# A new table of order, engine and PSUM bank for 2,542 operations of a four-layer attention kernel

## The chip, the cores and the metric

The kernel runs on one core of a Trainium2 chip. The metric is the device time of one execution in microseconds (us). The names of the engines are those of the profile: PE (TensorE matmuls), PEld (TensorE weight loads), DVE (VectorE), ACT (ScalarE), POOL (GpSimd) and SP (SyncE, which here only issues DMAs).

## The reference

Four layers run one after the other on x of 2048 tokens by 512 features. Each adds its result to x. Layers 1 and 3 are linear attention (A), layers 2 and 4 are causal attention in a window of 256 tokens (B), each with 32 heads of 16 features.

```python
def _A_ref(x, wqkv, wo):
    q, k, v = ...                      # x @ wqkv, split in 32 heads of 16
    phi = lambda t: jnp.where(t > 0, t + 1, jnp.exp(t)) + 1e-6
    pq, pk = phi(q), phi(k)
    kv = jnp.einsum("bhsd,bhse->bhde", pk, v)
    z = jnp.einsum("bhsd->bhd", pk)
    num = jnp.einsum("bhqd,bhde->bhqe", pq, kv)
    den = jnp.einsum("bhqd,bhd->bhq", pq, z)[..., None] + 1e-6
    o = num / den
    return ... o ... @ wo

def _B_ref(x, wqkv, wo):
    scores = jnp.einsum("bhqd,bhkd->bhqk", q, k) * (Dh ** -0.5)
    mask = (idx[:, None] - idx[None, :] >= 0) & (idx[:, None] - idx[None, :] < 256)
    p = _softmax(jnp.where(mask, scores, -1e9), axis=-1)
    o = jnp.einsum("bhqk,bhkd->bhqd", p, v)
    return ... o ... @ wo

x = x + _A_ref(_layernorm(x), A_wqkv, A_wo)
x = x + _B_ref(_layernorm(x), B_wqkv, B_wo)
x = x + _A_ref(_layernorm(x), A_wqkv, A_wo)
x = x + _B_ref(_layernorm(x), B_wqkv, B_wo)
```

## The kernel before

The 2048 tokens are 16 tiles of 128. x stays in SBUF (`xres`). A class `Plan` first writes down a graph of 2,542 operations. Each has a name, the engines that may run it, a function that emits its instructions, and what it reads and writes. One operation is a handful of instructions. The names that matter here:

- `x0` ... `x12`, `wAk`, `wAq`, `wAv`, `wAo`, `wBn`, `wBv`, `wBo` are the loads of x (by first tile) and of the weights, all issued by SP in `setup`. In the load list, the eighth and later ones wait for the load four places earlier in that list.
- `stats`, `aggr`, `eps`, `pow`, `xn` are the layer norm of a tile (DVE, and POOL for `pow`; `eps` on either). `T` brings the normalised tile into transposed form, by PE for a few tiles and by a DMA transposition on SP for the rest.
- `k`, `q`, `v` are the projections of an A layer, two operations a tile each; `E` (an exponential on ACT), `E1` and `phi` (DVE) follow on `k` and `q`. `g`, `gv`, `z`, `kv`, `kvm`, `M` form the state of an A layer; `den`, `rec`, `recb`, `spread`, `pqd` divide; `aout` and `res` close it.
- `bq`, `bk`, `bv` are the projections of a B layer. Their evacuations `bqe`, `bke`, `bve` may run on ACT or DVE. `kd` and `vd` are DMAs on SP that rearrange keys and values.
- `s` is a group of score matmuls into four PSUM banks, `ex` one of the two exponentials on ACT that read a pair of these banks, `mk` and `mf` the causal masks (DVE; `mf` on DVE or POOL), `pv` the product with the values, `rcp` and `div` the division, `oT` the transposition of the output, `bout` and `res` the end of the layer. There are 156 groups `s` and 312 `ex`.
- `outp` and `out` are the stores of the result, `outp` by POOL or SP.
- `fill` are ten dummy matmuls, `c..`, `zero`, `wp` are constants, clears and weight copies.

When the instructions are emitted, nothing is planned any more: `place` unpacks `TABLE`, a compressed string, and takes from it three things: one order of all operations, the engine of each operation that has a choice, and a PSUM bank for each of the 1,007 PSUM tiles. Each engine runs its operations in the order of the table, and waits with semaphores for what is not yet done. The core of it:

```python
order = [ops[raw[2 * k] + 256 * raw[2 * k + 1]] for k in range(n)]
...
    o.eng = ("PE", "ACT", "DVE", "POOL", "SP")[raw[2 * n + o.i]]
...
    x.banks = [raw[3 * n + k]]
```

An operation that opens a PSUM tile also waits for all users of the tile that held that bank before. SP executes its queue in order, so a DMA whose data isn't ready holds back the ones behind it. The DMAs that it has issued land later by themselves.

The score groups are emitted by `b_scores` (L638) and `b_far` (L677, L680). An `ex` (L648, L690) reads two banks with one instruction, through a view that steps from the first bank of the pair to the second. In the table before, the second bank of a pair is always the one after the first.

Of the kernel before, what the change touches and what calls it, by code (L numbers as in the profile page):

```python
# [11 lines left out]
P = 128  # L12
D = 512
DH = 16
S = 2048
T = 16
# [202 lines left out]
def bass_view(x, free):  # L219

    return bass.AP(x.tensor, x.offset, [x.ap[0]] + free)


class Plan:
# [398 lines left out]
    def b_scores(self, j, b, fs, key):  # L623

        K = self
# [4 lines left out]
        last = (q + ns - 1) // P  # L630
        span = lambda two, free: bass_view(K.PS[:, two[0].banks[0], :], free([512 * (two[1].banks[0] - two[0].banks[0]), 2]))

        def put(e):
            m = None
            for i, f in enumerate(fs):
                for gq in range(4):
                    rows = slice(32 * gq, 32 * gq + 32)
                    m = e.matmul(K.ps(ps[gq])[:, ns * i:ns * i + ns], K.kB[rows, j % 4, 2 * f + b, :, :], K.XQ[rows, f, q:q + ns], start=True, stop=True, tile_position=(32 * gq, 0))  # L638
            return m
# [5 lines left out]
        for h in range(2):  # L645
            def ex(e, h=h):
                i = span(ps[2 * h:2 * h + 2], lambda x: [[ns, n], x, [1, ns]])
                return e.activation(out(h, ns).rearrange("p (f g) c -> p f g c", f=n), i, ACT.Exp, bias=0.0, scale=0.25)  # L648

            self.on("ACT", "ex", ex, key + 0.01 * h, act(2 * ns * n), wr=[("P", sl, f, b, h) for f in fs], rd=[("P", sl, f) for f in fs], ps=[ps[2 * h], ps[2 * h + 1]])  # L650
# [9 lines left out]
    def b_far(self, j, key):  # L660
# [3 lines left out]
        ps = [Tile(1, "S") for _ in range(4)]  # L664
        span = lambda two, free: bass_view(K.PS[:, two[0].banks[0], :], free([512 * (two[1].banks[0] - two[0].banks[0]), 2]))

        def put(e):
            m = None
            for f in range(4):
                for b in range(2):  # L670
                    q = P * j + 64 * b
                    c = 128 * f + 64 * b
                    for gq in range(4):
                        rows = slice(32 * gq, 32 * gq + 32)
                        x = K.XQ[rows, f, q + 256:q + 320]
                        if not merged:
                            m = e.matmul(K.ps(ps[gq])[:, c:c + 64], K.kB[rows, j % 4, 2 * f + b, :, :], x, start=True, stop=True, tile_position=(32 * gq, 0))  # L677
                            continue
                        for half in range(2):
                            m = e.matmul(K.ps(ps[gq])[64 * half:64 * half + 64, c:c + 64], K.kB[rows, j % 4, 2 * f + b, 32 * half:32 * half + 32, :],  # L680
# [5 lines left out]
        for h in range(2):  # L686
            def ex(e, h=h):
                i = span(ps[2 * h:2 * h + 2], lambda x: [[128, 4], x, [64, 2], [1, 64]])
# [171 lines left out]
    r"c-qZa1K1|VvaT*P*0yciwr$(CZQHhO+qTW@CcDXcb7%hV<eVfoo0F4!@AKUGhSk+o?^{*fGyMUCh3765goc+c9E6835CI|rLPAiG2oggihztY|-3#}`C",  # L860
    r"4r=n43a|>hzijl3kWoa6p#`avO+fK1uY;ujD@Ez2SkS$&>LDpE9e8oAQe1v8a6_D$N)JZ7i0tjaUd=@c<fq38+hjCLu%LreIXx=gZ!`=YC|392gRX3jE",
    r"8s-6Ba;xXbbJY!USjp?I9C9aCKn-420Zp80tY9=m1@zK6Hc3&>dnyIY<i)AUHIJK`<CP!bC^_O<)o%ghj9zmcUi$1Y4j7Y=t3k1dhTn*aop79W;b4Py#",
    r"x`WOxo!U?>cOGEf$#LQi-BFJUPxgXItmuE7^L4%guZOoQoA9lpZPumWzvN{Fjw!EBfV!=XHU2d|(4Y=<4N6L!H|m;p0kHSC5}a023~lW+<^DHU4HgD@(",
    r"-N}%?_Ew~MLpedY&Gw>S1syz@+B~;(TS-1;7z#BLZ;Z=H72~d$@RTG*)26YbZ!F?D3BViO&1yK*+Eo4-gR3epF{Rlrn1Qk(5QUz5ZRaj+KSyU3G)k84K",
    r"s>rH{DypKWf=~#mKvb1fy@O;bxpFGH8VzHhw#urqsbVU-%Aty@5~`$%rgEyvkW!^kxl}1tTIE({RaI3@l~Gkx0jQ($KwhY;>Zt~*vZ}6XsFtdgYOQLjT",
    r"B^QU18ZR&6ow*D6xyhUs;z3I8mo4yiE6K!tBTN6HB&9rde{Ip-~#M}{cr#}sDm(CjZq=s5j=*uYM!bFW7Rk{QjJm<VVxSU)~iEM5+<mLYQDMzlhgur85",
    r"XJ|s-xPVp1@O>tlq;1n4)H=nQE3=q&BL>YKfYvrm5+wlez+%)Mm9`9aRU^QuPcvt1fDeI;OU$t?Hm!sk*9<uu9c})vBB7u0FvswOj?m;J8A~R=3n~6#|",
    r"2);OdSl1t-)=bxQS6Au$wQRoB#QbzN;!C9ouZhSMs9I;;+<N9wUEh1*p~6-t%H&=>}HsGaJGx~ZaL42+4-)C<*9mBF&OOYK(A)jf4zmBTZtmkNt})LB&",
    r";o~m=|fm)+3sEg{nTB~AX0!)Mn@uez{XYirAq-tU<ysK`gI2aG(Vr@K&=WrCB#|wB7M`IEkgYj{nN`|RaYV}UNS0B_H^-;Z5KdPTpQcR8^AsnVr;V}Y^",
    r"#c?<uBVt;W0uy5etcaDcGVWE8FeRo_bulug!i*RN>){oZ2`{S&I1w9Q6|9Q&F*9bt)OZPF;bp9Y)$o&QhAnV5&cV6Z96zf`_(gqHKP$jS*ch{7Hq4GW@",  # L870
    r"Gf4#?^Hv)hxf4wHpN#;AtK>xH5q?UQ*bJ_!mHQ@b7E_}hS#y2`d;-`jOA5Zte`5YN-7Q3z+9LXJ7X8@iVH9uw#0>)8@pk5%z$|?FXlr*jZrZ_7QjUq4H",
    r"u(9i%YNv&PRvKuqRH#7-}h|$CxUX>V*YyIZnqJ7+b|rE3go*!mYRsx8n|6iG5UGRUOyhIxLL+)Bx2RS7U!w1jEr<T#rSu7>1_^R2(BxB#KP)@EJbG7kC",
    r"4A;x62cd+-N*gEz4<RiU?d3m@SVe29;+5B9~ExEG^PRLY~OQa_AFc~yTLfcaE@)ebx0U7CdhaS%Sm0_q;M$4)pHhv1JGpAt|)x=#buAoU%-#u?NRXJR#",
    r"~PBo||?Zf@}3OC?Jyn_dDCVj%sIEyyn_qYXXQ40EkUvW0gp`Q^bB`HEmMX4zX#iH1hjN;Hx9ENGAHXX#Il$?g+2poy&XfAEW=oEuuQhjPb4=@8A!ozq3",
    r"(^5{#MYpjbJ)lhVkXlkkBFas9s1+rmN0gqJgftz+%(Rl)QXLwsT2mWpPl@RmKBgzMidIuQ>Oeo?dwhrSs4mr`yp)gf(+4a-9jOU5rB2kD3X-9&)Sa5qa",
    r"Xf(^@g#Pm=G2eYQGc38mK+76`LuxI(kVQR184&Ur$RK4TF`nbOkHRb^`IgYf{Icx8bpI>Ej^_nw3&v|7Ro|dX)6_{5>%2F(jr<+*=PxEqwTbmcF;1~NF",
    r"gZ{4N)W1P?eoRQy3~mKhPT*uHMoxwTpIB4%$PBI58*Tq@0Y`P-!YdWhpF`qsCO8l5+~~NiV4vrQ~NcjC#{|G@M4zNE$_r=oRgw*R-Gd&~y5p4$~2OL8I",
    r"v?9is#EiN4Sp9z$bkFYTnYypEgmJNiuTX&il}7Tl5#Q7S%8<LLyQq!08n0r&M@8mH(qt>?^~g@2-~oSJ{6kJO4=a~md3!)aNVIRuB~P@IF?a!wA-nhz3",
    r"kE<QtN=^UM>c07S5QXUS&VR;fwrYV$;^Ko7d$KkmM=jIEvfs1i|UQX$`D6gOl{3HLw@3=h|;6i+nE>UsL#+RuqZ{$rJfy;4cF3%OXAQ$G%+?Ts>f9}9t",
    r"xg!tcPW+xfa7C`fmH7%);eI@T2lF5v!iF7ZXUh>e5@+OK9GRnVRlZ8s=sNY_o*b2X@fIG*qj)Ms<7w1~qw{E<PJ4MD-=O^*gM0HwF2SF;6lda?e3Pnib",  # L880
    r"*{lRxg_u4ojjC>@h%R|lejcb=2~2v4{>*%!ee+Uf9B!5mACN--p;q^HXY_V+>MX$F+Ra{`3u+Mqdbj|b1aU{cPI`|=aYPnm0aK%tR*hbWRzK4hU0ld-~",
    r"gZJQ+$SvSUJtt`37I);1WXWa{~@34f!UY<=cFV@9<qd$WB5_SZT!fcs7TTIoz1%@;v^^;pIL@lwk5RXOrwQmO&!Od|to{c^v1EP_l@da8n-7&G-R7<VX",
    r"CNpKxS}BCVvgw2`B7iKEIfxy*YwJ}2Ob99?$vaY@LFc>*utrTj!#u5b*ACXwW+h=h|ka*gB4Q+~$FcsZ}&n37+f^9z0^&!wPT<=7HW;!6TaD7oZ?6p%!",
    r"cSdvI?$tx!$kDQcKa!$@mEGaBSWF@cS3sOifN^vPFB_*F+lFL#-DoST5A*=bNd?%HpvUHVV(q6hqDXAh=rJLlGYEoU=Nm5BB9i)czmX6X%l1p2uK(FMr",
    r"RHXirLQ+a9NiBV(uk@4er4n_Q9x^}%${_iH-*6g9D{r}{%$51lOXkS}dCA}LD}K%2b7?6ngJp=6k(x47W=Sn6FGFRRq?7bATjoePSt`q9xtx|Wa#m_f9",
    r"a$)grLNSI`qDt&$$R-A86>l;kd?AZ7ReGBE+b^5jFQo^R@TW6vR<;t8`&UN<f^QejFMHZiPCFiqr8<dGFCpyCut~+q_K>X@zO*#$#vN*TjYk^lv{FJ>g",
    r"xu2t8DXLX{5Ky4%sQqrG?y)rqWFA$^_XZtfz_SA7#4yB)eszOp-lvNHWP}nIU^+pG=W^GFA4=0ck1s<*+=EgYr<0$Rl|y_4H@?B3boU$)~gETsptbqx0",
    r"$l`ezBQL+Bhjx6Y|S7u4BwcCEG1g>*yRNEg<fbr)Sk57kyX-B>r#O?5L}R7cdqbXOflht-jEbKOF>)ZO$PJy#FcA$2R=PPf+`bVnUZch{|TC*4Mm(9?B",
    r"j9a;C#J#{bLTesDH^hg~{kJ91v3>`(!)1&nmT};o^vvhIYSC7>Lba*{bm(b(%AU#A6)=_mo-Csx0CG~h+T9?uj^h8}oZ_-<ISv_B0(O30m9mXus3-wmL",
    r"O@}qx^(1{w&(@3db-h@JGdJ{2eM>LV`}AZzMNiX3Oi@$J?AHhM4!ujS)wlId9p0?d>-8NSO&2#MOmrPXf2U*W*E*JdrDN+jI<Agjmg;3XqS>wY>VtZ@j",  # L890
    r";G`6je4qns-Njd=DFUWBbzAZrCy;|>OJ~<{YL+wALxgAmA<P#>d*R-KCBbyg!+j7q!a0qrj&W1SL=KFkiM_K=(r}Hd8>ca$Mp#v-yGGa^%;FqpVB|+$2",
    r"zJxs}t*UI-2>a-|2EXx+!fw==VCQPNI|P<hr~j<4rs!g-)pxnHVOC(dL+5qZ6B$rm9J5l9_5ImN~C~*2&EUeNls{pwXl=)lCL-NgHEL8B^9c6U?MHnM?",
    r"|k(xfuwOnH;hj5Xs-LQ~5mFi-S&)5r8R{Y)Lx-wZGVO?Fe;1UH#YYLnLFFgZ;wGsvVdgG~jK#nd(RO;%IUR5C+MJrlx&G@(p0)7<1X*-ReOz~nVGO)6c",
    r"*q}KV2GA&Fi)6z6D4NZDoQCHR(bX7gn3^Qr;Yg0*oZ>s2wdbnw9nwU)b2Q$KqG--8aolZA3Tg+Co&9pY#O&k;3j53qVQ8UHlHwDaOQ_!?Ag-l^H)l4(T",
    r"Obv6~yfK~4bTiL%F+0poQ`yWnNo-fs&5SV%%r3Lr>@jamQv0KsVP=_Rw!P_KCYnWNrdeo`+m7ZZv)H^d?@cFj%A7IPbazu-pEhkx9Xs08we{=-v)s%!b",
    r"IlyH!mKo_%mLHRoHZ$IeS6RxGKbAxv(Kco=gc*8-YhZ8%u=)8tTv&|8nf1{GpTG3)6?`a*Ud@Oz}C<=%uRE_T=JH8XvuysC(JE#(OfoH%x&}0tT&&`W&",
    r"PQFF{$lUbH`|V-#jp1%@K3gG_=+>vW@LM^UzD}Bjao^o5lvWkIfSk&PK3LO;(%DX1C#OTAR+Mw;}8^6Us)kA??owY$UtEY&4rpbQ{CQw4H2Z+u6plZEZ",
    r"Un+IF#Ft=KS@Z3f%kX0(}X6Wi2AvAJv>+srn%(QFIb()Kp3Y;OD9<hA*1ew*1wwXtm+8`s9O#cXl=!n`!!nG&|9uBGeh0(Od>YU}7}wxBI!YwM+UnVoL",
    r"C+8H*B&1rMk<@Sv2X3yGlwy^DPi`toXmYr?m+XVKNNob4Mezw0IU`yIkw!E!i=h)IVkzHk1+cLJYtzs+MO16g`XxG?5wyLdWhuib^f^B0j+FtgOoonaW",
    r"`L?I+ZTs30cChVZJJ`$Cy0vz_9ckCuQP#O3Hkb?U7TAThwcTd7+eP-Sy=TkW9X5~KU^m*1_P)*Qs@obigv;kbx=^mB-DDrxC$^RyZO7QncDK#%3b@Dii",  # L900
    r"rr#w*qgSXE9A=Bv38tYVsF`%cB>t4huNq0ncZWb+ZFZ)`__hbyX+nN#$L78>|uM|zOXy(Ui;F9ar^CJd&Iu7-`Vf&YkSllu*d8J`_M*p2kjwy-2P}|x!",
# [169 lines left out]
```

## Time and profile before

| what | value |
| --- | --- |
| time, median of 3 runs | 410.4 us (410.2 to 413.33) |
| span of the profiled execution | 408.2 us, 18,082 instructions, granted clock 1.000 |
| what the lowest run has beyond this span | 410.2 - 408.2 = 2.0 us |
| PE, PEld, DVE, ACT, POOL busy | 396.0, 263.4, 347.9, 344.4, 113.8 us |
| first and last `ex` of layer 2 | 62.7 to 224.4 us |
| first and last `ex` of layer 4 | 257.6 to 400.7 us |
| DMA | 37.88 MB, mean 93 GB/s |

The time of a run is a little longer than the span, which goes from the first to the last instruction of the profiled execution. Layer 1 lies ahead of the first `ex`, layer 3 mostly between 213 and 258 us, where few exponentials of scores run. A busy PE is not a PE at its peak, since matmuls are pipelined and their ends are modelled.

### The profile page before, as it was taken

The numbers are of one execution on the slowest core, as the hardware profiler recorded it, in microseconds if no ns is written. First come the engines' busy times: TensorE is split into PE (matmuls) and PEld (weight loads), VectorE is DVE, ScalarE is ACT, GpSimd is POOL, SyncE is SP. The second block draws the span as 40 slices with busy tenths as digits, with TensorE's granted clock in tenths as the row PEclk, the third lists the DMA queues.
The fourth block names the chain that finished last, engine by engine and source line by source line (L and its number), as shares of the span: only waits on it lengthen the run. The fifth ranks groups of instructions, "written<-read, shape, count | busy, mean of one in ns | idle before, by whom it ended". The sixth has DMA issues, their size and how long they took to land.

```text
span 408.2 us, 18082 instructions
## 1 busy us (share of the span) xinstructions
PE 396.0 (97%) x7997; PEld 263.4 (65%) x7997; DVE 347.9 (85%) x808; ACT 344.4 (84%) x443; POOL 113.8 (28%) x194
## 2 busy tenths in 40 slices
PE   8999999999999999999999999999999999999996
PEld 3654676666575566666666777676757766576664
DVE  5998799999998999888977789988898778876685
ACT  3655579999999999999998355999998999999992
POOL 3553632112253343330503202122123201302212
PEclk9999999999999999999999999999999999999999
DMA  8754014923242934344231100364225542442543
GB/s 247 243 118 104 2 42 121 184 56 97 65 119 52 132 73 108 75 104 106 62 69 36 29 2 28 89 127 78 71 76 130 143 83 61 66 121 62 118 109 104
DMA packets 67654, 37.88 MB, mean 93 GB/s; under 512 B 48248, under 2 KB 62712, under 8 KB 67576
## 3 DMA queue, kind: packets, MB, share of 16 engines
q1 hardware_dynamic: 67184, 35.67, 38.1%
q8 instruction: 63, 1.03, 1.1%
q0 software_dynamic: 384, 1.05, 0.8%
q14 instruction: 15, 0.12, 0.1%
q10 hardware_dynamic: 8, 0.00, 0.0%
HBM read 6.29 MB, written 2.10 MB: 21 GB/s over the span
## 4 chain that ended last, share of the span: by engine, by line
PE 81%; ACT 10%; DVE 7%; DMA 1%; issue 1%; DVEq 0%
PE ps L406 27%; PE ps L420 20%; PE ps L729 15%; PE ps L638 8%; ACT pb L648 7%; PE ps L680 2%; PE ps L481 2%; ACT pb L690 1%; DVE XQ L563 1%; PE ps L677 1%; DMA XQ<-vp 1%; PE ps L984 1%; PE ps L457 1%; PE ps L543 1%; PE ps L268 1%
## 5 line engine op out<-in xcount | busy, mean ns | idle before, releaser
L648 ACT ACTIVATE pb<-ps 128x1024 bf16<-128x1024 f32 (+3 forms) x224 | 198.2, 966 | 7.4 <-PE ps L638 6.2
L729 PEld LDWEIGHTS ps<-vB,pb 128*128 128x128 bf16 x2560 | 77.6, 96 | 11.5 <-issue 4.2
L729 PE MATMUL ps<-vB,pb 128*128 128x34 bf16 x2560 | 83.2, 177 | 0.3
L420 PE MATMUL ps<-xT,wBp 128*128 128x128 bf16 x1024 | 68.6, 219 | 0.1
L420 PEld LDWEIGHTS ps<-xT,wBp 128*128 128x128 bf16 x1024 | 58.4, 98 | 9.6 <-issue 4.0
L708 POOL TENSOR_SCALAR_AFFINE_SELECT pb<-pb 128x1024 bf16<-128x1024 bf16 x34 | 39.1, 1149 | 84.0 <-DVE pb L700 31.9
L429 ACT ACTIVATE tE<-ps 128x512 bf16<-128x512 f32 x64 | 38.1, 606 | 18.4 <-PE ps L406 12.1
L638 PE MATMUL ps<-XQ,kB 32*128 32x256 bf16 (+2 forms) x1024 | 48.7, 262 | 3.3 <-ACT pb L648 0.6
L574 DVE TENSOR_TENSOR xres<-ps,xres 128x512 bf16<-128x512 f32 x63 | 43.1, 685 | 9.6 <-PE ps L406 9.1
L690 ACT ACTIVATE pb<-ps 128x1024 bf16<-128x1024 f32 x50 | 49.0, 1048 | 1.3 <-PE ps L680 1.0
L406 PE MATMUL ps<-wA,XQ 128*128 128x512 bf16 x192 | 49.2, 380 | 0.7 <-DMA XQ<-vp 0.6
L369 POOL TENSOR_SCALAR ve<-mv 128x1 f32<-128x1 f32 x49 | 11.8, 240 | 127.9 <-DVE mv L368 126.9
L370 POOL TENSOR_TENSOR rs<-ve,negh 128x1 f32<-128x1 f32 x64 | 37.9, 592 | 32.0 <-DVE ve L369 27.5
L367 DVE BATCH_NORM_STATS2 stats<-xres 128x6 f32<-128x512 bf16 x64 | 43.8, 685 | 2.8 <-DMA xres<-in_A_x_dram 2.1
L638 PEld LDWEIGHTS ps<-XQ,kB 32*128 32x128 bf16 x1024 | 15.7, 92 | 31.4 <-ACT pb L648 8.3
L420 PE MATMUL ps<-XQ,wA 128*128 128x128 bf16 x512 | 34.4, 219 | 0.0
L406 PE MATMUL ps<-wBv,xT 128*128 128x512 bf16 x128 | 34.3, 380 | 0.0
L406 PE MATMUL ps<-M,XQ 128*128 128x512 bf16 x128 | 33.3, 380 | 0.2
L420 PEld LDWEIGHTS ps<-XQ,wA 128*128 128x128 bf16 x512 | 30.1, 98 | 5.1 <-issue 0.6
L406 PE MATMUL ps<-wBo,oT 128*128 128x512 bf16 x124 | 32.7, 380 | 0.6 <-DVE vp L431 0.4
L656 DVE TENSOR_TENSOR pb<-pb,tri 128x512 bf16<-128x512 bf16 x68 | 27.7, 419 | 3.7 <-ACT pb L648 3.1
L741 DVE TENSOR_TENSOR o<-ps,rc 128x256 bf16<-128x256 f32 x64 | 27.0, 422 | 1.7
(114 smaller groups left out, 545.9 us busy)
## 6 DMA issues: line engine op xcount, KB each, us to landing
vB<-vS SPq DMA_DIRECT2D x64, 136.0 KB, 2.6
kB<-vp SPq DMA_DIRECT2D x64, 128.0 KB, 2.2
wA<-in_A_wqkv_dram SPq DMA_DIRECT2D x3, 512.0 KB, 5.2
xres<-in_A_x_dram SPq DMA_DIRECT2D x2, 512.0 KB, 4.8
pb<-in_B_wqkv_dram SPq DMA_DIRECT2D x1, 1024.0 KB, 6.9
out_dram<-xres POOLq DMA_DIRECT2D x8, 128.0 KB, 2.5
out_dram<-xres SPq DMA_DIRECT2D x7, 128.0 KB, 2.0
xres<-in_A_x_dram SPq DMA_DIRECT2D x3, 256.0 KB, 5.3
```

The lines of the kernel that those rows point to most:

```text
L367: self.on("DVE", "stats", lambda e: e.bn_stats(K.stats[:, t, :], K.xres[:, t, :]), key, dve(512), rd=[("xres", t)], wr=[("stats", t)])
L370: self.pow = self.on("POOL", "pow", lambda e: e.tensor_tensor(K.rs[:, t, :], K.ve[:, t, :], K.negh[:], ALU.pow), key + 0.03, (640, 690), r ...
L406: m = e.matmul(K.ps(ps), lhs(c), rhs(c), start=c == 0, stop=c == 3)
L420: m = e.matmul(K.ps(ps)[:, f * P:(f + 1) * P], w(c, f), xT(c), start=c == 0, stop=c == 3)
L429: self.on("ACT", "E", lambda e: e.activation(K.tE[:, s, :], K.ps(ps), ACT.Exp, bias=0.0), key, act(512), wr=[("tE", s)], ps=[ps])
L574: self.on("DVE", "res", lambda e: e.tensor_tensor(K.xres[:, t, :], K.ps(po), K.xres[:, t, :], ALU.add), key, dve(512), rd=[("xres", t)], w ...
L638: m = e.matmul(K.ps(ps[gq])[:, ns * i:ns * i + ns], K.kB[rows, j % 4, 2 * f + b, :, :], K.XQ[rows, f, q:q + ns], start=True, stop=True, ti ...
L648: return e.activation(out(h, ns).rearrange("p (f g) c -> p f g c", f=n), i, ACT.Exp, bias=0.0, scale=0.25)
L656: return e.tensor_tensor(x, x, K.tri[:, 0, :].unsqueeze(1).to_broadcast([P, 4 * n, 64]), ALU.mult)
L690: return e.activation(o.rearrange("p (f g) b c -> p f g b c", g=2), i, ACT.Exp, bias=0.0, scale=0.25)
L708: return e.affine_select(out=x, in_=x, compare_op=ALU.is_ge, fill=0.0, base=-2, pattern=[[0, 16], [-2, 64]], channel_multiplier=1)
L729: m = e.matmul(K.ps(ps)[:, 34 * u:34 * u + 34], K.P((b // 2) % rp)[:, f, gq % 2 * 2 + gq // 2, o:o + P], K.vB[:, (b // 2) % 4, b % 2, r, : ...
```

## The change

Only the table is new, and one helper that goes with it. In the new table, the two banks of an `ex` may come in either order, so the bank with the lower number is sorted to the front, both where the matmuls write and where `ex` reads:

```diff
--- before.py
+++ after.py
@@ -628,6 +628,7 @@   (b_scores)
+        two = lambda h: sorted(ps[2 * h:2 * h + 2], key=lambda x: x.banks[0])
         span = lambda two, free: ...
@@ -635,7 +636,7 @@
-                    m = e.matmul(K.ps(ps[gq])[:, ns * i:ns * i + ns], ...)
+                    m = e.matmul(K.ps(two(gq // 2)[gq % 2])[:, ns * i:ns * i + ns], ...)
@@ -644,7 +645,7 @@
-                i = span(ps[2 * h:2 * h + 2], lambda x: [[ns, n], x, [1, ns]])
+                i = span(two(h), lambda x: [[ns, n], x, [1, ns]])
...                          (the same three edits in b_far)
 TABLE = (
-    r"c-qZa1K1|VvaT*P*0yciwr$(CZQHhO+qTW@CcDXcb7%hV<eVfoo0F4!@AKUGhSk...
+    r"c-qxj1Jo?ZlFkfdWM130ZQHhO+qP}nwr$(C?U{S;R{j6X*_qipvomks?m1iC)m0...
...
 )
```

Unpacked by the same lines of `place`, the two tables compare so:

| | before | after |
| --- | --- | --- |
| operations, PSUM tiles | 2,542, 1,007 | the same |
| operations on PE, ACT, DVE, POOL, SP | 868, 442, 807, 190, 235 | 868, 445, 802, 190, 237 |
| operations that change engine | | 61 |
| PSUM tiles in another bank | | 820 |
| `ex` whose two banks are in falling order | 0 of 312 | 50 of 312 |
| changes of the PE's tile mode | 333 | 334 |
| `mf` on DVE, POOL | 17, 39 | 15, 41 |
| of these in layer 4 | 13, 15 | 9, 19 |
| `eps` on DVE, POOL | 15, 49 | 13, 51 |
| `outp` on POOL, SP | 8, 7 | 6, 9 |
| `bqe`, `bke`, `bve`, `ve` on ACT | 10, 7, 7, 5 | 9, 8, 8, 6 |
| `recb` on ACT, DVE | 5, 3 | 3, 5 |

The order of the first DMAs on SP, before and after:

```
before  x0 x1 wAk x2 x4 wAq x6 x8 wAv x12 wBn T5 T6 T7 wAo T8 T9 T10 T11 T13 T12 T14 T15 wBv ... wBo (37th)
after   x2 x0 x1 wAq x4 x6 wAk x8 x12 wBn T5 T6 T7 T8 T9 T10 wAv T11 T13 wAo T12 T14 T15 wBo wBv ...
```

(T5 is the transposition of tile 5 in layer 1.) The order on PE in the first microseconds, where `fill` is left out: before T0, T1, k0, k1, q1, T2, q0, T3, k2, T4; after T0, T1, T3, q0, then k0 with T2 inside, k1 with q1 inside, T4, k3.

On PE, the score groups come in the same sequence at 154 of the 156 places. Between one score group and the next, the same operations stand in 92 of the 156 stretches. At the end, the two `bout` of tile 13 move from between the last score groups to behind the last `pv`, and the last two score groups swap places.

## The prediction

> **What bounds the kernel now.** I read the page first, then busy time by stretch, then what ACT waits for, then the chain and the DMAs at the start.
>
> ```profile
> PE 396.0 (97%) x7997; PEld 263.4 (65%) x7997; DVE 347.9 (85%) x808; ACT 344.4 (84%) x443; POOL 113.8 (28%) x194
> PE 81%; ACT 10%; DVE 7%; DMA 1%; issue 1%; DVEq 0%
> ```
>
> PE looks full, and the chain that ended last is 81% PE. But the row stretches over pauses: if every PE operation is given the median distance from its start to the next start among its kind, the 868 operations sum to 374.4 us, so some 34 us of the 408.2 are not matmul work: 5.3 ahead of the first real one (nine warming matmuls until 5.27), the rest small pauses inside "busy". The stretches say where another engine sets the pace. I chose their edges at the first score exponential of layer 2, the end of its dense part, layer 3 and the halves of layer 4.
>
> ```profile
> 62.70:213.60 150.90, 148.83 (x3026) 96.94 (x3027) 135.80 (x319) 147.72 (x171) 44.77 (x67) 1.00 0.44 95
> 224.40:257.60 33.20, 33.10 (x528) 24.77 (x526) 29.00 (x64) 16.52 (x30) 5.71 (x11) 1.00 0.10 26
> 257.60:329.00 71.40, 71.10 (x1718) 50.47 (x1717) 61.16 (x143) 67.19 (x85) 17.20 (x24) 1.00 0.45 99
> 329.00:400.70 71.70, 67.41 (x1825) 46.02 (x1823) 55.88 (x126) 68.47 (x85) 12.10 (x16) 1.00 0.39 89
> ```
>
> Columns after the length: PE, PEld, DVE, ACT, POOL. ACT is busy 147.7 of 150.9 us in layer 2 and 135.7 of 143.1 us in layer 4, but only 16.5 of 33.2 in layer 3. So ACT and PE pace the B layers together, handing PSUM banks to and fro, and PE alone paces the A layers. What a better order can win in a B layer is the time in which ACT stands still: 3.2 us in layer 2, 7.4 us in layer 4. In layer 4 the waits are mostly for score groups that PE reaches late:
>
> ```profile
> ACT pb L648 <- PE ps L638: 3.2, 7, 0.7
> ACT vp L648 <- PE ps L638: 1.8, 4, 0.6
> ACT pb L690 <- PE ps L680: 1.0, 5, 0.3
> ```
>
> **The start.** Seven loads of 2 MB in all lead the queue in both versions, in other order. Issue times are 1.72 (wAk), 3.33 (wAq) and 3.85 us (x6); the times to landing, asked in narrow windows, are:
>
> ```profile
> wA<-in_A_wqkv_dram SPq DMA_DIRECT2D x1, 512.0 KB, 5.0
> wA<-in_A_wqkv_dram SPq DMA_DIRECT2D x1, 512.0 KB, 6.3
> xres<-in_A_x_dram SPq DMA_DIRECT2D x1, 256.0 KB, 6.5
> xT<-xn SPq DMA_TRANSPOSE x1, 5.3
> ```
>
> So they land at 6.7, 9.6 and 10.4 us, in the order of issue. After, wAk is the seventh: the same 2 MB end with it, so it lands at about 10.4 instead of 6.7. x0 comes behind x2; 256 KB more took 0.7 us (from x2 to x4), so the first `stats`, at 2.86 before, starts near 3.6, of which `eps` on DVE gives back 0.2. PE is held by wAk. Before, the first k ran at 7.72. After, T0, T1, T3, all ten fills and q0 come first, and k0 starts at 10.4. From there to the first `g` stand 12 operations of k (a pair takes 0.86, row of 4 matmuls of L406 in the chain), 6 of q (0.45 each) and 2 transpositions (0.22): 5.2 + 2.7 + 0.4 = 8.3, so 18.7 us. Before, the first `g` came at 16.48 with three operations of k and one of q fewer done (1.7 us), so at 18.2 for the same work. The start costs 0.5 us. Bounds: -0.2 (fills that now cover the wait leave no other hole) and +1.2 (x0's delay of 0.7 comes on top).
>
> Next comes the only DMA on the chain:
>
> ```profile
> 30.23 0.34 DVE stats L367
> 30.57 4.23 DMA XQ<-vp
> 34.80 0.04 issue
> 34.84 1.47 PE ps L406 x6
> ```
>
> This is the transposition of tile 12, and PE waited 0.59 us for it. After, the load wAo (512 KB) stands right ahead of it. A transposition behind such a load (wBo, at 71.4) took 5.3 us, another 1.8 us behind one took 2.9, the median is 2.5 to 2.6. I take a landing at 35.5 to 36.7 instead of 34.8. PE has two more operations of `g` (0.86) to do ahead of it and comes 0.5 later, so it waits 0 to 1 us where it waited 0.6. The layer then ends 0.3 us later, with bounds of -0.6 (the slow 4.23 was an accident, and all is hidden) and +1.3. wBo itself leaves the busy time at 70.8 for the quiet time near 40; the transpositions that it held (up to 2.9 us) had delayed no PE instruction there, so I count nothing; it is a point for the first rival.
>
> **The B layers.** ACT's work. In layer 2 up to the 144th `ex`: one E less (0.606), one `bve` more (0.672), one `bqe` less (0.597): -0.5 us. In layer 4: one `bke` more (0.755), one `recb` less (0.307): +0.4. Together -0.1. PE's work does not change, and its mode changes go from 333 to 334. What is left is how evenly PE's work lies between score groups. I summed, for each stretch from one score group to the next, PE's work in it less ACT's work that covers it, where positive, with the durations above (an ACT instruction occupies 0.12 less than its row, from 4 `ex` in 3.77 us). Layer 2 goes from 5.8 to 6.6 us, layer 4 from 7.5 to 6.9. The waits measured are 2.5 and 7.2, so the measure is of the right size. It gives +0.2. Bounds: -0.6 and +0.8, if only one layer's change is real. The single waits agree: those at 308.8 (0.63), 326.4 (0.57), 335.8 (0.48) and 338.0 (0.49) have the same neighbours after; those at 314.8 (0.52) and 386.5 (0.68) lose the `bout` pair in front; in exchange layer 2 has seven stretches with a surplus over 0.3, where it had three. B layers: +0.1.
>
> The 61 changes of engine lie off this: `mf` and `eps` go between DVE (135.8 of 150.9 busy) and POOL (28% over the kernel). `mf` takes 0.69 on DVE and 1.145 on POOL, and its product `pv` is the loop with the most room: the shortest way from a score group through `mf` to `pv` holds 4.1 us of PE work in both orders. Were that cover gone, each of the four that move to POOL in layer 4 would cost 0.46, 1.8 in all. The queue of SP: counted in PE work between producer and consumer, DMAs with less than 1 us to spare go from 7 to 5, less than 2 us from 25 to 24. No new wait there, 0. Layer 3 keeps its work and PE its 100%: 0.
>
> **One rule against row.** Masks that overlap a POOL mask:
>
> ```profile
> L656 DVE TENSOR_TENSOR pb<-pb,tri x68: 360/418/502, 70.1 to 396.4; 128x512 bf16<-128x512 bf16 x68
> ```
>
> The longest mask is 0.502 us, 0.08 over the median. By this row, four more POOL masks in layer 4 cost DVE 4 x 0.08 = 0.3 us, all hidden, and I count that. The Trainium skill (SBUF — State Buffer, section SBUF: two separate sides) says that a DVE instruction with two SBUF inputs and a GpSimd instruction share a port pair under an exclusive lock, and the loser blocks for the whole instruction. By that rule the four would hold DVE for up to four whole POOL masks; the trace shows no such hold.
>
> **The end.** The `bout` pair of tile 13 leaves the front of the last `pv` (0.86 earlier there) and comes behind it, before the last `bout` (0.86 later). 0, bounds -0.9 (the copies of `oT` hid only behind the pair of tile 14) and +0.9 (the front waits for the last exponential anyway). Of the last stores one moves from POOL to SP, 0.59 of issue beside `res` of 0.69: hidden, 0.3 if not.
>
> **Sum** against the span of 408.2: 0.3 + 0.1 + 0 = +0.4, so 408.6. The median of the runs is 2.2 us above the span, so 410.8.
>
> **Rivals.** First: **fewer waits**. The orders differ most in which operation fills a hole, and an order that suits many landing times may close what one landing time opens. If half of the waits of ACT in the B layers (2.5 + 7.2 = 9.7) and the 0.6 at 34.8 go, it is -5.5 and 404.9; if all go, -10.3 and 400.1. For it: wBo out of the way, fewer tight DMAs. Against it: DMA is 1% of the chain, and the four largest unchanged waits.
>
> Second, slower: **shorter bank loops**. Place: PE in both B layers, at an `s` that must wait until `ex` has emptied its banks, while `pv`, `bq` and `bout` queue behind it and then ACT starves. The PE work between a score group and the next one that opens one of its banks has a median of 2.02 us before and 1.80 after; two `ex` of 0.92 need some 2. The shortfalls against 2 us sum to 88.9 before and 93.8 after. Most of it is hidden because ACT still has the other pair; if all of the difference comes on the path it is +4.9, so 415.3. It decides from the point where ACT has no second pair in store. Against it: the surplus measure hardly moves.
>
> Third, slower too: **the masks hold DVE**. If each of the four POOL masks more in layer 4 stops a DVE mask for its whole 1.145 us (row L708), and the `pv` behind it waits, it is 4.6 us, so 415.0. Against it: the longest mask of 0.502 us.
>
> That the table does nothing at all can't be: 820 tiles change banks.
>
> **How the numbers follow.** Forecast 0.44, fewer waits 0.31, bank loops 0.20, masks 0.05. No change within 1% (4.1 us, about what a measurement of this kernel can tell from no change) is the forecast, with its own range from 410.4 - 0.6 - 0.6 - 0.9 = 408.3 to 410.4 + 1.3 + 0.8 + 0.9 + 0.3 = 413.7. Faster is the first rival, slower the other two. The range reaches down to two thirds of the first rival's 10.3, 403.5, and up to the second's 4.9 with the start's upper 1.2, 416.5.
>
> **What would show it.** After: the first k near 10.4 and the first `g` near 18.7; a wait of 0 to 1 us for tile 12 near 35; the first score exponential near 63; ACT idle in layer 2 near 3.5 and in layer 4 near 7; the same PE and ACT sums. Wrong would be a layer 4 shorter than 141 us or longer than 146, an `s` that waits more than 1 us for a bank, or DVE masks over 0.6 us.

## The result, and the profile after

| | before | after |
| --- | --- | --- |
| median of the first runs | 410.44 us (4 runs) | 416.94 us (4 runs, 415.55 to 417.99) |
| ratio, 95% interval | | 1.0140 [1.0098, 1.0182] |
| a second set, on one chip | 410.25 us (11 runs) | 415.10 us (6 runs, 413.15 to 417.97) |
| ratio, 95% interval | | 1.0134 [1.0101, 1.0167] |
| profiled execution, its span | span 408.2 us | 416.36, 414.6 us; in the second set 413.15, 411.4 us |

The change makes the kernel 1.4% slower by the ratio. The forecast of 410.8 us, no change, did not come: the medians lie 6.5 us (first runs) and 4.9 us (second set) above those of before.

Two profiles of the changed kernel exist, and they are used side by side, since they differ by 3.2 us. First the rows of the page and the stretches of the first one. 68 of its 7,997 matmul records are missing, which lowers its PE sum (389.3; the second profile, with all records, has 398.1); the weight loads are all there.

```profile
PE 389.3 (94%) x7929; PEld 263.6 (64%) x7997; DVE 344.6 (83%) x803; ACT 347.0 (84%) x446; POOL 113.4 (27%) x194
PE 66%; ACT 12%; DVE 10%; DMA 9%; issue 2%; SPq 1%; POOL 0%; POOLq 0%
```

The engines have nearly the same work. The chain does not: DMA goes from 1% to 9% of it, PE from 81% to 66%. The stretches (PE, PEld, DVE, ACT, POOL after the length) follow those of before. Two edges differ: the third stretch begins 1.4 us behind the last exponential of layer 2 (228.1), and the last one ends 0.4 us behind the last exponential of all (405.6):

```profile
10.00:20.00 10.00, 7.05 (x69) 4.34 (x68) 8.60 (x27) 6.21 (x12) 5.48 (x14) 1.00 0.67 205
67.10:218.70 151.60, 145.18 (x2985) 96.57 (x3013) 135.56 (x317) 147.31 (x170) 43.15 (x66) 1.00 0.43 91
229.50:263.00 33.50, 32.74 (x499) 24.36 (x503) 28.96 (x65) 17.58 (x31) 3.71 (x9) 1.00 0.09 22
263.00:335.00 72.00, 69.84 (x1704) 50.53 (x1717) 60.43 (x139) 67.46 (x85) 20.60 (x28) 1.00 0.42 93
335.00:406.00 71.00, 65.79 (x1826) 45.72 (x1833) 53.37 (x124) 67.99 (x85) 15.13 (x19) 1.00 0.46 100
```

Layer 2 has 151.6 us where it had 150.9, and layer 4, up to its last exponential, 142.6 where it had 143.1. ACT stands still for 4.3 us in layer 2 (3.2 before) and 7.2 in layer 4 (7.4 before). Most of the loss is not there. It begins in the first line: between 10 and 20 us PE works 7.05 of 10 us. Before, it worked all of them:

```profile
10.00:20.00 10.00, 10.00 (x102) 6.69 (x100) 10.00 (x31) 6.75 (x13) 5.56 (x15) 1.00 0.79 250
```

The trace gives the start of every instruction, and the table says which operation it belongs to. So each profile can be cut into parts from operation to operation:

| part, us | before | after, first | after, second |
| --- | --- | --- | --- |
| first k | at 7.50 | 11.15 | 12.03 |
| first `g` | at 16.26 | 21.58 | 20.18 |
| first score group (the start) | at 62.29 | 66.66 (+4.37) | 65.41 (+3.12) |
| layer 2, to its 73rd score group | 151.30 | 152.03 (+0.73) | 151.64 (+0.34) |
| layer 3, to the first score group of layer 4 | 43.41 | 43.74 (+0.33) | 43.72 (+0.31) |
| layer 4, to the last `pv` | 144.80 | 144.31 (-0.49) | 143.61 (-1.19) |
| last `pv` to the last `res` | 3.88 | 5.41 (+1.53) | 4.57 (+0.69) |
| sum | 405.68 | 412.14 (+6.46) | 408.94 (+3.26) |

The start makes two thirds to nearly all of it. What PE waited for up to 45 us in the first profile names its parts (us in total, times, longest):

```profile
PE ps L406 <- DMA XQ<-vp: 2.4, 2, 1.5
PE ps L383 <- DVE vp L371: 1.3, 2, 0.8
PE ps L406 <- DMA wA<-in_A_wqkv_dram: 0.9, 1, 0.9
```

These are the transpositions T5 (1.5) and T12 (0.9), the normalised tiles for T0 and T4 (0.8 and 0.5), and wAk. Before, PE waited 0.6 us in this time, for T12 alone. (The wait ahead of its very first matmul, 1.2 us, is the same in both.) The difference is 4.0 us. Another 0.4 is work in another order: the new table has two operations of `q` more and one `aout` less ahead of the first score group. Together that is the 4.4 of the table above. The chain of waits shows the longest of them (start, length, what):

```profile
4.34 8.25 DMA xres<-in_A_x_dram
...
12.61 0.70 DVE stats L367
13.31 0.31 DVE vp L371
...
13.65 6.34 DMA XQ<-vp
...
20.04 0.60 PE ps L406 x2
...
34.21 5.37 DMA XQ<-vp
...
39.72 1.46 PE ps L406 x6
```

DVE waits for the load x8 until 12.59, does the `stats` of tile 8, and only then `xn` of tile 5 (the 0.31). The 1 MB load wBn, which also waits for x8, is issued at 12.61. The transposition T5 is issued behind it at 13.65 and lands 6.3 us later. PE has k of tile 5 ahead of the first `g`, and stands. The same comes again at 34.21 with T12 behind wAo. The end of the first profile, again from the chain:

```profile
405.42 3.85 DMA oT<-o
...
409.32 1.04 PE ps L406 x4
410.36 0.88 PE ps L777 x6
```

And of the second:

```profile
402.52 2.63 PE ps L731 x96
...
405.27 0.86 PE ps L406 x4
...
407.16 0.88 PE ps L777 x6
```

In the first, `bout` of tile 14 (409.32) waits for the transposition of its `o`; in the second that has landed in time and PE runs through.

### The profile page after: what moved, and what is told of

The parts are those of the page before. It is cut to its first block, busy times and chain, and to the rows that moved or that the text cites. A ratio compares the mean times of both kernels' runs of the same rounds, so it can differ in the third digit from the quotient of the medians.

```text
span 414.6 us, 18034 instructions
## 1 busy us (share of the span) xinstructions
PE 389.3 (94%) x7929; PEld 263.6 (64%) x7997; DVE 344.6 (83%) x803; ACT 347.0 (84%) x446; POOL 113.4 (27%) x194
## 4 chain that ended last, share of the span: by engine, by line
PE 66%; ACT 12%; DVE 10%; DMA 9%; issue 2%; SPq 1%; POOL 0%; POOLq 0%
PE ps L406 22%; PE ps L420 16%; PE ps L731 12%; ACT pb L649 8%; PE ps L639 7%; DMA XQ<-vp 3%; DMA xres<-in_A_x_dram 2%; DMA xT<-xn 2%; PE ps L481 2%; PE ps L682 2%; ACT pb L692 2%; DVE stats L367 1%; DMA vB<-vS 1%; DMA oT<-o 1%; PE ps L457 1%
## 5 line engine op out<-in xcount | busy, mean ns | idle before, releaser
L710 POOL TENSOR_SCALAR_AFFINE_SELECT pb<-pb 128x1024 bf16<-128x1024 bf16 x37 | 42.9, 1159 | 70.0 <-DVE pb L702 18.8
L406 PE MATMUL ps<-wA,XQ 128*128 128x512 bf16 x178 | 47.3, 379 | 5.3 <-DMA XQ<-vp 2.4
L639 PE MATMUL ps<-XQ,kB 32*128 32x256 bf16 (+3 forms) x1024 | 48.1, 262 | 3.1 <-ACT vp L692 0.5
L406 PE MATMUL ps<-wBo,oT 128*128 128x512 bf16 x108 | 29.6, 380 | 3.0 <-issue 0.8
L406 PE MATMUL ps<-wBv,xT 128*128 128x512 bf16 x107 | 29.3, 379 | 2.9 <-issue 1.6
L657 DVE TENSOR_TENSOR pb<-pb,tri 128x512 bf16<-128x512 bf16 x68 | 29.3, 441 | 3.1 <-ACT pb L649 3.1
L406 PE MATMUL ps<-M,XQ 128*128 128x512 bf16 x113 | 30.2, 380 | 1.6 <-issue 0.8
L742 DVE RECIPROCAL rc<-ps 128x16 f32<-128x16 f32 x64 | 16.1, 252 | 17.8 <-PE ps L731 17.3
```

Of the source, the lines that this page charges most:

```text
L406: m = e.matmul(K.ps(ps), lhs(c), rhs(c), start=c == 0, stop=c == 3)
L639: m = e.matmul(K.ps(two(gq // 2)[gq % 2])[:, ns * i:ns * i + ns], K.kB[rows, j % 4, 2 * f + b, :, :], K.XQ[rows, f, q:q + ns], start=True, ...
L657: return e.tensor_tensor(x, x, K.tri[:, 0, :].unsqueeze(1).to_broadcast([P, 4 * n, 64]), ALU.mult)
L710: return e.affine_select(out=x, in_=x, compare_op=ALU.is_ge, fill=0.0, base=-2, pattern=[[0, 16], [-2, 64]], channel_multiplier=1)
```

## The experiments

The theory: the start's new order of loads, DVE and PE makes 3 to 4.4 us, the end the rest, and the B layers nothing. The rival: waits in layers 2 and 4, shorter bank loops among them. All kernels below differ from these two in the table alone. Where a table is put together from two, some operations near the cut come in an order that neither table has.

**The whole start, there and back.** Two kernels exchange everything up to the first score group.

```diff
 head_before: engines, banks and order of the changed table
-  operations up to the first score group as after
+  operations up to the first score group as before
 head_after: the reverse, on the table before
```

> The changed table, but the operations up to the first score group (some 62 us: loads, transpositions and projections of layer 1) in the order and with the engines and banks of the table before. Start theory (the loss of 6.5 us, 410.4 to 416.9, is made by late transfers of the first 40 us, 4.4 us at the first score group by the two traces): some 412.5 us, the first score group near 62.3 us of the span. Rival (waits in layers 2 to 4, shorter bank loops among them, make most of it, and the late start would be caught up or replaced by them): 415.5 us or more.

Measured: 414.89 us (4 runs; ratio 1.0100 [1.0068, 1.0133]), first score group at 62.41, profiled execution 413.4 us.

> The table before, but the operations up to the first score group in the order and with the engines and banks of the changed table: the reverse of the run beside it. Start theory: 410.4 + 4.4 = 414.8 us, the first score group near 66.7 us. Rival (layers 2 to 4): 410.5 to 411.5 us, a late start being caught up by the layers behind it.

Measured: 415.28 us (1.0105 [1.0067, 1.0142]), first score group at 66.58. In this second one all score groups from there to the 139th come 3.9 to 4.3 us later than before: the loss of the start goes through the layers almost undiminished. (The last ones come 6.2 later, behind a fall of the granted clock; see the end.) By the medians the new start alone costs the kernel before 5.0 us, as much as the whole change costs in its second set.

Taking the new start back out of the changed kernel gains less. The first kernel falls between its two expectations: by its profile it gains 3.0 us against the first profile of the changed kernel. By its median it gains 2.0 us against the first runs and only 0.2 against the second set, not 4.4. Three of its four runs had a mean granted clock of 0.995 or 0.996; the one at 1.000 took 413.4 us, 1.8 less than the changed kernel at the full clock (415.2, below).

The layer 2 of that kernel takes 153.03 us, 1.0 more than in the first profile. So with an early start the rest of the new table costs some 2.5 us more than before in layers 2 to 4. Whether that is the new order itself or the cut in the table is not settled. In the profiles of the changed kernel, e5, e6, e9 and e12, where those layers are uncut, they cost between -0.6 and +0.7; in e3 and e10, whose profiles ran at a clock of 0.996 and 0.995, +1.7 and +1.0. The size of the start's loss is thus shown in one direction, and open in the other.

**Parts of the start.** Each kernel is the changed table with moves in the queue of one engine. In the cuts the number behind a name is its tile (k5 k5 are the two operations of k of tile 5), and `...` stands for what is left out.

> The changed table with only the first seven loads of the queue in the order before (x0, x1, wAk, x2, x4, wAq, x6 instead of x0 behind x2 and wAk seventh). If the order of the loads makes the late start: the first k group near 7.7 us instead of 11.2 and 412.5 to 413.5 us. If it is the transposition of tile 5, issued behind the 1 MB load wBn and behind a statistics that waits for x8 (the first g at 21.6 us): the first k comes early, TensorE then waits longer for tile 5, and the time stays within 1 us of 416.9.

```diff
 SP (e3)
-x2 x0 x1 wAq x4 x6 wAk
+x0 x1 wAk x2 x4 wAq x6
```

Measured: 417.32 us (414.86 to 420.78; 1.0171 [1.0104, 1.0238]); the time says little, three of the four runs having a mean granted clock of 0.992 to 0.996. In the trace wAk lands early, but the first k comes at 10.59, because on PE it stands behind T3, whose x2 now lands later (6.89 instead of 3.58). First `g` 20.30, first score group 65.34. Neither expectation came. The load order put back alone does not repair the start; how much of the loss is its own this run cannot tell.

```diff
 SP (e5)
-x12 wBn T5 T6 ... wAo T12
+x12 T5 wBn T6 ... T12 wAo
```

> The changed table with two loads moved on SP's queue and nothing else: the 1 MB load wBn from ahead of the transposition of tile 5 to right behind it, and the 512 KB load wAo from ahead of the transposition of tile 12 to right behind it. Theory (a transposition lands only when the load issued just ahead of it has): tile 5, issued at about 13.65 us, lands near 16.2 instead of 20.0, the wait of k of tile 5 (1.9 us) goes and the first g comes near 19.7 instead of 21.6; tile 12 lands near 37 instead of 39.7 and its 1.2 us of wait go; the first score group comes near 63.6 to 64.5 instead of 66.7, and the time is 414 to 415 us. Rival (the transpositions are late for their own sake, 16 DMA engines being full with x8 and x12 as well): tile 5 still lands at 19 or later, the first g within 0.5 us of 21.6, and the time within 0.7 us of the changed kernel's 416.9.

Measured: 415.03 us (1.0112 [1.0073, 1.0152]), first `g` 19.62, first score group 64.59. T5 landed at 17.39, not near 16.2 as expected, but in time: the wait for it is gone, and PE works 9.95 of the 10 us in which T12 had stopped it. The stretches from 30 to 40 us, first the changed kernel:

```profile
30.00:40.00 10.00, 9.08 (x60) 4.75 (x60) 8.07 (x23) 3.55 (x6) 3.96 (x10) 1.00 0.78 156
```

Then e5:

```profile
30.00:40.00 10.00, 9.95 (x57) 4.73 (x57) 8.03 (x23) 4.07 (x7) 3.81 (x10) 1.00 0.73 144
```

```diff
 PE (e12)
-k5 q2 k4 k5 g0 g1 g2
+q2 k4 g0 g1 g2 k5 k5
```

> The changed table with one pair moved on TensorE: k of tile 5, which waited 1.9 us for its transposition ahead of everything else, behind the first three g products and the last q and k of tiles 2 and 4. No load and no transposition is moved: tile 5 still lands about 0.5 us behind wBn. Theory (the loss there is the order on TensorE together with the late landing): the first g at 18.9 to 19.4 instead of 21.6, no wait for tile 5 over 0.3 us, the first score group 1.3 to 1.9 us earlier than in the changed kernel's first profile (64.8 to 65.4), 414.3 to 415.5 us. Rival (the g products wait for VectorE's feature maps in that place, so that the wait only changes its name): the first score group within 0.6 us of 66.7, 416 us or more.

Measured: 413.71 us (1.0106 [1.0044, 1.0167]), first `g` at 18.63, first score group 64.51, a little better than the theory had it. Nothing in the DMA queue was touched, and T5 landed at 19.15, nearly as late as in the first profile.

```diff
 DVE (e9)
-stats8 xn5 aggr stats6 xn4
+xn5 aggr stats6 xn4 stats8
```

> The changed table with one move: the statistics of tile 8, for which VectorE waits until the load x8 has landed at 12.6 us, behind the normalizations of tiles 5 and 4 instead of ahead of them. Two theories of the wait in line: (a) the wait for x8 and the late landing of tile 5 behind wBn stand one behind the other in such a way that the second hides the first: tile 4 is transposed earlier (from 14.65 to about 13.0), but tile 5 still lands near 20, the first g stays within 0.4 us of 21.6 and the time within 0.5 us of the changed kernel's; (b) they add: the first g 0.9 us or more earlier, and 416.0 us.

Measured: 416.19 us (1.0154 [1.0112, 1.0197]), T4 at 13.26 instead of 14.65, first `g` 20.80, and the piece of the chain is there again:

```profile
12.48 6.73 DMA XQ<-vp
```

The landings settle which theory holds:

| profile | wBn issued, landed | T5 issued, landed | first `g` |
| --- | --- | --- | --- |
| before | 11.84, 18.72 | 17.03, 19.54 | 16.26 |
| after, first | 12.61, 19.47 | 13.65, 19.99 | 21.58 |
| after, second | 11.71, 16.96 | 12.75, 17.50 | 20.18 |
| e9, `stats` of tile 8 late | 12.07, 18.73 | 12.48, 19.21 | 20.80 |
| e12, k5 behind `g` | 11.74, 18.66 | 12.79, 19.15 | 18.63 |
| e5, wBn behind T5 | 14.69, 20.09 | 13.35, 17.39 | 19.62 |

In the four rows where T5 was issued behind wBn within about 1 us, it lands 0.5 us after it, whether that is 4.7 or 6.7 us after its own issue. In e9 the first `g` came 0.8 us earlier, where (a) allowed 0.4 and (b) asked for 0.9, so its number falls between. But the 0.8 is what wBn itself landed earlier (19.47 to 18.73), and wBn was issued earlier because x8 had landed earlier (12.05 instead of 12.59), which DVE's order doesn't touch. By the landings theory (a) holds. With T5 landing at like times, k5 behind the `g` (e12) has its first `g` 2.2 us earlier than e9. Before, T5 also landed behind wBn, but k5 stood behind the first `g` products, so nobody waited. The load, the transposition behind it and PE's order make this wait together; moving the transposition (e5) or k5 (e12) removes it. It is not the whole loss of the start: in both kernels the first score group still comes 2.2 to 2.3 us later than before. In e12 PE waits 1.0 us for T0, 0.4 for T4 and 1.0 for T12, in all 2.4 where it waited 0.6 before. With the 0.4 of work in another order that is the 2.2.

**The end.**

> The changed table with its last operations (from about 390 us on: the last score groups, the second-last and last pv, the bout of tiles 13 and 14, the last store) in the order before. Tail theory (the pv of tile 14 put behind a score group leaves the transposition of its o no slack: bout of tile 14 waits until 409.3): 1.5 us less than the changed kernel, 415.4 us. Rival (the end is set by the last exponential alone, whose place both have alike): within 0.4 us of 416.9.

> The table before with the end (from the score groups of the last row on, 396.7 us) in the order of the changed table: larger score group first, pv of tile 14 behind it, bout of tile 13 behind the last transposition. Theory (the gain at the last pv, 0.9 us, is given back because the transposition of o of tile 14 starts 1.4 us later and the copy of the last o waits for bout of tile 13, whose buffer it takes): from the last exponential to the end 1.5 us longer, last pv 0.9 earlier, together +0.6: 411.0 us. Rival (the end follows the last exponential and pv): 0.5 to 0.9 us less than before, 409.6.

```diff
 PE (e4: to the upper order, e7: to the lower)
-pv14 pv14 s bout13 s bout13 pv15 x4 oT bout14 ...
+pv14 s pv14 s pv15 x4 oT bout13 bout13 oT bout14 ...
```

Measured: 416.05 us (1.0129 [1.0099, 1.0160]) and 412.34 us (1.0044 [1.0021, 1.0068]). Neither time shows what it was to show, because each cut brought a wait of its own ahead of the end: 1.0 us in the first, 1.4 in the second, where a score group waits for the bank of an earlier `pv`. Eight of the ten runs of e7 also had a mean granted clock under 0.997. The parts of the profiles do show it. From the last `pv` to the last `res`, e4 takes 3.88 us, as before, instead of 5.41. e7 takes 5.05, and the stretch from the third-last score group to the last `pv` goes from 5.07 to 4.09. So the new end wins 0.9 to 1.0 at the last `pv` and pays 0.7 (in the second profile of the changed kernel) to 1.5 behind it. The chain of e7:

```profile
400.77 3.49 DMA oT<-o
...
404.30 1.04 PE ps L406 x4
```

**Two tries at a repaired start, and one at a better kernel.**

```diff
 e6: e5, and
 SP   -x2 x0 x1 wAq x4 x6 wAk       +x0 x1 wAk x2 x4 wAq x6
 DVE  -stats3 aggr3 stats2 xn1      +stats2 xn1 stats3 aggr3
 DVE  -stats8 xn5 ... xn4           +xn5 ... xn4 stats8
 PE   -T3 q0 q0 k0                  +k0 k0 T3 q0 q0
```

> The run beside it with three further moves: the first seven loads in the order before, the statistics of tile 2 behind the normalization of tile 1 and those of tile 8 behind the normalization of tile 4 on VectorE, and k of tile 0 ahead of the transposition of tile 2 on TensorE. If load order, in-order VectorE and the two large loads are all that the start lost, the first score group comes at 62.3 to 63.0 and the time is 412.5 us, as with the whole start of before. If something else of the start's order (engines, banks, the order of g and k) costs as well, it stays above 64.

Measured: 414.41 us (1.0099 [1.0069, 1.0130]), first score group 64.85, no better than e5. The edit missed its aim: of the statistics that wait for x2 it moved those of tile 3, and those of tile 2 stayed ahead of `xn` of tile 1, where DVE waited 2.0 us.

```diff
 e10: e6, and
 DVE  -stats2 xn1 stats3            +xn1 stats2 stats3
 DVE  -stats7 xn5 stats6 xn4 stats8 +xn5 xn4 stats7 stats6 stats8
 PE   -k0 k0 T3 q0 q0 T2 k1         +k0 k0 k1 k1 q0 q0 T3 T2
```

> The second try at a repaired start. In the first, the first score group stood at 64.85: VectorE had the statistics of tile 2 ahead of the normalization of tile 1 and waited there 2.0 us for the load x2, since only those of tile 3 had been moved. Now the statistics of tiles 2 and 3 stand behind the normalization of tile 1, those of tiles 7, 6 and 8 behind that of tile 4, and k of tile 1 and q of tile 0 ahead of the transposition of tile 3; the two large loads as in the other runs. Theory (what is left of the start's loss is VectorE waiting in order for loads): first score group at 63.0 to 63.8, 412.5 to 413.5 us. Rival (it is something else of the start's order): 64.5 or later, 414.4 us.

Measured: 417.30 us (1.0158 [1.0124, 1.0193]), first score group 67.27, worse than unrepaired. k of tile 1, moved forward, waited for the copy of T1, and that stood on ACT behind a constant copy that waited for POOL (behind this wait the granted clock fell too; see the end):

```profile
PE ps L406 <- ACT XQ L390: 3.6, 1, 3.6
```

So the last 2.2 us of the start, between e12 (64.5) and before (62.3), are named as waits (1.8) and as work in another order (0.4), but no kernel here is without them.

```diff
 PE, table before (e8)
-g k12 ... g g      pv s      (three places)
+g g g k12 ...      s pv
```

> The table before with four small moves on TensorE: two g products (tiles 10 and 11) ahead of the first k of tile 12, which waits 0.96 us for its transposition at 33.9 us, and three score groups each ahead of one pv (at 308.4, 326.0 and 385.4 us, where ScalarE stood idle 0.6 to 0.8 us for them). Theory (a saving in layer 1 reaches the end undiminished, as its loss did, and ScalarE's gaps in layer 4 are TensorE's order): first score group at 61.4 to 61.7, 0.6 to 0.9 us less from the first move and up to 1.8 us from the others: 408.0 to 409.7 us. Rival (the gaps are refilled behind, TensorE being the bound in layer 4): only the first move counts, 409.6 us; or nothing, 410.4.

Measured: 411.04 us (12 runs; 1.0024 [0.9993, 1.0054]). First score group 62.05, a gain of 0.24 instead of 0.6 to 0.9. Behind the score groups put forward, 0.9 us was lost from 306 to 330 us: the gaps did not close but moved, ACT's gap at 326.4 growing from 0.57 to 0.91. The theory falls. Of the rival its last form is left: nothing gained. No version beat the kernel before.

**The changed kernel again.**

> The changed kernel once more, for more times of it beside the others: both theories 416 to 417 us, with the first score group near 66.6; the question is how much of the 6.5 us between the medians goes with the granted clock, which stood at 0.995 in two of its four runs, 1.8 us slower than the other two, and at 0.998 to 1.0 in nearly all runs of the kernel before. If half of its runs again have 0.995 or 0.996, some 0.9 us of the loss of the median is the clock's.

Measured: 415.10 us, first score group 65.41. T5 landed 2.5 us earlier than in the first profile, since wBn was issued 0.9 us earlier and took 5.2 us instead of 6.9, and PE worked through:

```profile
10.00:20.00 10.00, 10.00 (x107) 6.88 (x106) 9.25 (x28) 7.01 (x12) 5.65 (x15) 1.00 0.66 202
```

It lost at another place: T0 came at 7.34, because DVE has `stats` of tile 1 ahead of `xn` of tile 0, and x1 landed at 5.84 (5.01 in the first profile, 3.54 before). Behind T0 stand six `fill`. In the first profile they take 1.5 us:

```profile
6.74 1.46 PE L268 MATMUL ps<-kB 128*128 128x512 bf16 x6
```

In the second they run at about half that rate:

```profile
7.74 2.74 PE L268 MATMUL ps<-kB 128*128 128x512 bf16 x6
```

So T1, whose tile was ready at 8.99, started behind them at 9.88, and k of tile 0 later still. Of ten runs of the changed kernel, seven with a mean granted clock of 0.999 or 1.000 have a median of 415.2 us, three with 0.995 or 0.996 have 418.0. So at the full clock the loss is 5.0 us. In the first runs the two at the full clock have 416.0, so the clock's share of that median is about 1 us.

## Why the prediction was wrong where it was

**The start: the step that failed**, +0.3 forecast at the end of layer 1 and +3.1 to +4.4 measured.
- wAk's landing, 10.4, was near: 11.1 and 10.2. The first k came at 11.15 on that landing. In the second profile it came at 12.03, since T0 was later than the 0.7 us allowed (1.0 us in the first, 1.8 in the second) and the `fill` behind it ran slowly. I had x0 behind x2 in the sum, but not that DVE wants x1 as well before it finishes tile 0. (The 7.72 and 16.48 that the sum names for before are the ends of what ran ahead; the first k and the first `g` started at 7.50 and 16.26.)
- From there to the first `g` I summed 8.3 us of PE work and let nothing wait in it. The work was right: 8.15 us in the second profile, where PE does not wait. In the first it took 10.4, with 0.9 us lost ahead of T4 and 1.9 ahead of k5 (counted from start to start; the rows above, which count from the modelled end of a matmul, have 0.5 and 1.5). I counted the k operations that had come ahead of the first `g` as work of 0.43 each, and never asked when T5 lands for k5, although T5 stands right behind wBn in both lists of DMAs. Before, T5 was issued 5.2 us behind wBn, after 1.0 us, and both times it landed behind it. e12 puts k5 back and has its `g` at 18.63. That it meets the 18.7 of the forecast is chance: it has two operations of k (0.86) fewer ahead of the `g` and loses about as much on the way.
- T12: the row chosen was right (5.3 us behind a 512 KB load; 5.37 came), the start was not: it was issued at 34.21 and landed at 39.6, not at 35.5 to 36.7, as everything ahead was late. PE lost 1.2 us on it from start to start (0.9 by the rows).

The two chains of loads were taken one by one, each hidden or small. A sum of expected values does not hold where an in-order engine waits for the later of several landings.

**The B layers**, forecast +0.1, with bounds of -0.6 and +0.8 for layers 2 and 4. Layers 2 and 4 together gave +0.2 in the first profile and -0.9, a little under the lower bound, in the second; layer 3 gave +0.3 for a forecast of 0. About right; e1 with its +2.5 is the exception left open. ACT idle came as said (4.3 and 7.2 for 3.5 and 7).

**The end**, forecast 0 as -0.86 and +0.86. The first term came to 0.90 (from the 151st score group to the last `pv` 9.40 us before, 8.50 in both profiles). The second was 1.53 and 0.69, above the bound of 0.9 in the first profile. What I missed: `pv` of tile 14 comes behind a score group, so its transposition is issued 1.31 us ahead of the last `pv` instead of 2.69, and the copy of the last `o` needs a buffer that `bout` of tile 13 now frees late.

**The rivals.** Bank loops named a time near the result (415.3), but not its cause: no `s` waits over 0.5 us for ACT by the matmul rows (0.8 by the weight loads), and the start of after alone costs the kernel before 5.0 us (e2). Fewer waits did not come. The range reaches up to 416.5 only by the 4.9 of these bank loops; that the measured 415.1 and 416.9 lie about its upper end is luck.

**The rule against the row** went to the rule. In the changed kernel masks are held:

```profile
L657 DVE TENSOR_TENSOR pb<-pb,tri x68: 355/415/1173, 75.2 to 402.4; 128x512 bf16<-128x512 bf16 x68
L702 DVE TENSOR_TENSOR pb<-pb,tri x44: 358/415/967, 270.3 to 395.8; 128x512 bf16<-128x512 bf16 x44
L702 DVE TENSOR_TENSOR vp<-vp,tri x12: 412/418/752, 298.7 to 381.5; 128x512 bf16<-128x512 bf16 x12
```

Five masks take 0.68 to 1.17 us, in both profiles and at the same operations. Each began while a POOL mask ran, and ended 0.27 us after that one's end. The Trainium skill (SBUF — State Buffer, section SBUF: two separate sides) says just that: whichever of the two starts first has the ports for its whole instruction. The longest mask of 0.502 that I set against it was no counterexample: before, only four of these `mk` masks met a POOL mask at all, two of them came first, and two began 0.2 us before it ended. And the trace of before does show such a hold, in a row that I did not set beside it, that of `mf` on DVE:

```profile
L709 DVE TENSOR_TENSOR pb<-pb,tri x16: 627/682/882, 90.1 to 396.8; 128x1024 bf16<-128x1024 bf16 x16
```

The one of 0.88 us began at 356.9, 0.35 us before a POOL mask ended. So the sign that I had named for being wrong, a mask over 0.6 us, came. Its price did not: the five add 2.7 us to DVE, three of them lie in layer 2, and the chain runs on PE at those places. That this cost nothing is read from the chain, not tried.

## What to carry to other kernels

Where an order is changed ahead of a stretch of loads, write down for every DMA what stands in front of it in its queue, when the bytes ahead of it will have landed, and which in-order engine needs it first; a transposition right behind a load was here as late as that load. Then ask what is behind that waiting instruction: here the same late landing cost nothing with k5 behind three `g`, and nearly 2 us ahead of them. The longest value of a row says what happened in one order of things, not what can happen in another.

## What the runs showed of the hardware

- The DMAs of SP's queue landed in the order of issue in the profiles of this case, as far as issue and landing can be matched. Behind wBn, T5 landed 0.5 us after it in the table above, but 2.0 and 2.1 us after it in e3 and e4; T12 landed 0.5 to 0.6 us after wAo. From issue to landing these took 4.7 to 6.7 us, where most transpositions of layer 1 with no load right ahead took 2.4 to 2.9. Not all did: T12 of the kernel before took 4.2 and T5 of e5 4.0, for a reason that stays open. The 1 MB load took 5.2 and 6.9 us in two executions of one and the same table, and with it the wait ahead of the first `g` went or came.
- The granted clock (the third number from the right in a stretch) fell in places. In e10 it did so after PE had stood 3.6 us for the copy of T1:

```profile
8.00:12.00 4.00, 0.56 (x3) 0.06 (x1) 2.67 (x8) 1.41 (x2) 2.10 (x6) 1.00 1.00 330
12.00:16.00 4.00, 3.81 (x26) 2.60 (x27) 2.70 (x6) 0.19 (x2) 1.27 (x4) 0.57 0.30 58
```

In e2, near the end, it fell after a pause of only 1.3 us:

```profile
392.00:396.00 4.00, 4.00 (x73) 1.95 (x69) 2.26 (x7) 3.45 (x5) 0.00 (x0) 0.62 0.41 90
```

Of 50 runs of the kernel before beside the experiments (a 51st, of 1188.9 us, is left out), 5 had a mean clock under 0.997, of 71 runs of all other tables 29. What in a table brings it about stays open.
